# Attention with a long convolution in one kernel: score matmuls in tiles of four heads, a ring of three score bank pairs, and an instruction order planned at build time

## The chip, the cores and the metric

The kernel runs on one core of a Trainium2 chip. The metric is device time in microseconds (us). The engines are PE (TensorE, the matmuls), PEld (its weight loads), ACT (ScalarE), DVE (VectorE), POOL (GpSimd) and SP (SyncE, which issues most transfers). PSUM is the memory for the results of matmuls; both kernels use it as eight banks of 512 f32 columns. The "granted clock" is the share of full speed that TensorE was given in a stretch of time. In the traces of the kernels before and after, every record of it is 0.5 or 1.0; these are the low and the high clock below.

## The reference, cut to what matters

```python
# x: [2048, 640] bf16; 32 heads of 20; one key head and one value head for all
def A(q, k, v, shift_k, ssm_k, ssm_D):        # gated long convolution
    kv = shift_conv_4_taps(k, shift_k) * v
    y  = irfft(rfft(kv, 4096) * rfft(ssm_k, 4096))[:2048]   # causal convolution
    return q * (y + kv * ssm_D)
def B(x, wq, wk, wv, wo):                     # attention, 32 query heads
    p = softmax((x @ wq) (x @ wk)^T * 20 ** -0.5)           # 32 x 2048 x 2048
    return (p @ (x @ wv)) @ wo
g = sigmoid(sum(x * gate_w))
out = g * A(x, ...) + (1 - g) * B(x, ...)
```

The 32 x 2048 x 2048 exponentials are 1024 ScalarE instructions of 128 x 1024 elements, before and after. A head has 20 columns. A 21st carries a subtracted bound, so that no row maximum is needed, and the value matrix has a column of ones, so that the sum of the exponentials comes out of the output matmul. The trace lists a full matmul as `128*128` (rows and columns of the array), a score matmul as `21*128` and an output matmul as `128*32`. A score matmul therefore needs 21 of 128 rows. An output matmul needs 32 of 128 columns.

## The kernel before

Two heads form an item. There are two score slots (banks 0 to 3), two buffers ET for exponentials and two output banks (4 and 5). While the exponentials run, all other matmuls share banks 6 and 7.

```python
def QK(n):                                    # two heads: two row tiles
    ss = n % 2
    for hl in range(2):
        r = 2 * (hp % 2) + hl
        bankno = 2 * ss + hl
        op("pe", matmul(self.bank(bankno, 0, 512), A["kT4"][32*r:32*r+21, ...],
                        A[f"qT{g}"][32*r:32*r+21, ...], tile_position=(32 * r, 0)), ...)
# ... EXP(n): one activation over both banks of the slot into ET[n % 2]
# ... PV(n): two column-tiled matmuls, ET[n % 2] x vaug into bank 4 or 5
for n in range(N):                            # N = 1024
    EXP(n)
    if n + 2 < N:
        QK(n + 2)
    PV(n)
    # ... at the end of a head group: NORM, and OPROJ at the end of a query block
    self.step_credit += self.per_item         # convolution steps, evenly by weight
    self.step_credit = pull_steps(self.step_credit)
```

The convolution is done in blocks of 512 rows. Its steps take a spectrum of a block of kv again for each output block that needs it:

```python
for fc in range(4):
    for dl in range(b + 1):                   # output block b needs kv blocks b, b-1, ..., 0
        units.append((b, dri, d0, dn, fc, dl))
# ... each unit: X_unit(i = b - dl): 4 + 4 matmuls, two evacuations, then the products
```

All projections, the shifted product k * v and the gate came ahead of the first exponential. The spectra of ssm_k did too, in part.

## Time and profile before

| | before |
|---|---|
| time, median of 3 runs | 1838.95 us (1837.67 to 1840.55) |
| profiled span | 1834.4 us |
| first / last exponential starts | 247.1 / 1809.0 us |
| mean granted clock | 0.621 |

The main lines stand in the prediction below. Two more views help. The first is the chain of work that ended last, followed back from the end, as shares by engine:

```profile
PE 45%; ACT 17%; POOL 14%; DVE 13%; issue 9%; DMA 2%; SPq 0%; ACTq 0%; POOLq 0%; DVEq 0%
```

The second is a table by stretches: window, its length, then busy time (and number of instructions) of PE, PEld, DVE, ACT and POOL, the granted clock, the share of the DMA engines and GB/s.

```profile
0.00:247.00 247.00, 126.23 (x622) 48.87 (x622) 117.93 (x253) 56.15 (x81) 29.02 (x28) 0.70 0.13 39
247.00:647.00 400.00, 333.63 (x1455) 90.24 (x1455) 140.34 (x215) 246.67 (x246) 243.81 (x204) 0.67 0.10 29
647.00:1047.00 400.00, 355.71 (x1330) 79.90 (x1331) 99.76 (x143) 273.12 (x268) 82.57 (x105) 0.55 0.01 2
```

The chain is mostly PE. The stretches show how a kernel can be "bound by PE" and still lose time elsewhere. In the first 247 us no engine is much over half busy and no exponential runs. After that PE is 83 to 89% busy and ACT 62 to 68%.

### The profile page before, as it was taken

Reading aid. Unit: us, or ns where it says so; the run is one execution under the profiler, and the core shown is the slowest. Engines: PE = TensorE matmul, PEld = TensorE weight load, DVE = VectorE, ACT = ScalarE, POOL = GpSimd, SP = SyncE. Lnnn points to the kernel's source line nnn. Section 1 sums busy time; section 2 is a strip of 40 time slices with the busy share of each in tenths; the row PEclk is TensorE's granted clock in tenths of the full one; section 3 lists DMA queues with packets and bytes.
Section 4 is the critical chain, followed back from the end, with each engine's and each line's share of the span. In section 5 each row is a group of like instructions: output and inputs, shape, how many; then the busy total and the mean of one; then the engine's idle time right before and its main releaser. Section 6 shows DMA issues by size and latency. Waiting matters only on the chain.

```text
span 1834.4 us, 16661 instructions
## 1 busy us (share of the span) xinstructions
PE 1498.4 (82%) x6154; PEld 387.7 (21%) x6154; DVE 602.8 (33%) x1009; ACT 1091.1 (59%) x1105; POOL 599.2 (33%) x651
## 2 busy tenths in 40 slices
PE   3767258989968678999989888888989898898896
PEld 2212112212212122111111222221212211222221
DVE  6223842222355551212121233222315532323223
ACT  1213246756746437777767567666666466777674
POOL 1000199990056651102204044422234214524220
PEclk7787565655868676555555685655555756567556
DMA  3000222210000000000000000000000000000000
GB/s 109 1 0 1 79 72 72 72 45 10 4 1 1 0 8 8 0 1 0 1 0 1 8 8 1 1 0 0 1 1 1 15 1 0 1 1 1 1 1 15
DMA packets 22591, 24.70 MB, mean 13 GB/s; under 512 B 3316, under 2 KB 22382, under 8 KB 22510
## 3 DMA queue, kind: packets, MB, share of 16 engines
q1 hardware_dynamic: 22510, 23.64, 4.2%
q8 instruction: 48, 0.79, 0.2%
q14 instruction: 33, 0.27, 0.0%
HBM read 21.02 MB, written 2.62 MB: 13 GB/s over the span
## 4 chain that ended last, share of the span: by engine, by line
PE 45%; ACT 17%; POOL 14%; DVE 13%; issue 9%; DMA 2%; SPq 0%; ACTq 0%; POOLq 0%; DVEq 0%
ACT ET L1034 16%; PE ps L1024 13%; PE ps L1048 13%; PE ps L775 7%; POOL ksh_t L631 4%; POOL ksh_t L628 4%; PE ps L884 3%; PE ps L710 3%; POOL U L804 2%; DVE ps L1065 2%; POOL mtmp_pool L804 2%; POOL kv L635 1%; POOL ksh_t L624 1%; DVE accsb L1058 1%; PE ps L1075 1%
## 5 line engine op out<-in xcount | busy, mean ns | idle before, releaser
L1034 ACT ACTIVATE ET<-ps 128x1024 bf16<-128x1024 f32 x1024 | 1034.9, 1024 | 532.3 <-PE ps L1048 503.5
L1024 PE MATMUL ps<-qT,kT 21*128 21x512 bf16 x2048 | 562.0, 545 | 102.0 <-ACT ET L1034 71.9
L1048 PE MATMUL ps<-ET,vaug 128*32 128x512 bf16 x2048 | 569.0, 553 | 0.7 <-ACT ET L1034 0.7
L783 DVE CAST Xs<-ps 128x512 bf16<-128x512 f32 (+1 forms) x160 | 77.0, 489 | 500.5 <-PE ps L775 470.5
L804 POOL TENSOR_TENSOR mtmp_pool<-Xs,Kspec 128x128 f32<-128x128 bf16 (+3 forms) x189 | 146.7, 776 | 277.6 <-DVE U L804 265.9
L1024 PEld LDWEIGHTS ps<-qT,kT 21*128 21x128 bf16 x2048 | 102.8, 97 | 535.8 <-ACT ET L1034 433.3
L1048 PEld LDWEIGHTS ps<-ET,vaug 128*32 128x32 bf16 x2048 | 104.4, 99 | 390.5 <-issue 388.9
L897 POOL TENSOR_TENSOR yp<-yp,yp 128x512 bf16<-128x512 bf16 (+1 forms) x32 | 26.4, 825 | 458.3 <-DVE yp L888 457.6
L804 POOL TENSOR_TENSOR U<-U,mtmp_pool 128x128 f32<-128x128 f32 (+1 forms) x180 | 152.3, 846 | 14.1
L1065 DVE RECIPROCAL ps<-ps 128x512 f32<-128x512 f32 x32 | 107.7, 3367 | 21.6 <-PE ps L1062 21.6
L775 PE MATMUL ps<-kv,Tcos 128*128 128x512 bf16 (+1 forms) x320 | 88.0, 420 | 28.6 <-DVE Xs L783 22.6
L775 PE MATMUL ps<-kv,Tsin 128*128 128x512 bf16 (+1 forms) x320 | 89.3, 426 | 16.1 <-DVE oT L1067 14.6
L804 POOL TENSOR_TENSOR U<-Xs,Kspec 128x128 f32<-128x128 bf16 (+1 forms) x32 | 28.8, 901 | 205.5 <-DVE AB L846 204.2
L624 POOL TENSOR_TENSOR ksh_t<-kslab,w_all 128x640 bf16<-128x640 bf16 x16 | 22.8, 1423 | 212.1 <-DMA kslab<-in_A_k_dram 212.1
L246 DVE CAST Kspec<-ps 128x512 bf16<-128x512 f32 (+1 forms) x64 | 31.5, 491 | 173.6 <-PE ps L594 173.6
L248 ACT ACTIVATE qT<-ps 128x512 bf16<-128x512 f32 x32 | 18.6, 592 | 105.3 <-PE ps L710 89.3
L888 DVE CAST yp<-ps 128x512 bf16<-128x512 f32 (+1 forms) x32 | 15.7, 490 | 196.8 <-PE ps L884 196.8
L628 POOL TENSOR_TENSOR ksh_t<-kslab,w_all 128x640 bf16<-128x640 bf16 x48 | 68.7, 1431 | 2.5
L631 POOL TENSOR_TENSOR ksh_t<-ksh_t,ksh_t 128x640 bf16<-128x640 bf16 x48 | 67.6, 1409 | 3.8
L1058 DVE COPY accsb<-ps 128x512 f32<-128x512 f32 x32 | 22.1, 689 | 132.9 <-PE ps L1048 132.9
L1075 PE MATMUL ps<-wo,oT 128*128 128x512 bf16 (+1 forms) x256 | 49.7, 355 | 17.4 <-DVE outsb L1081 12.6
L884 PE MATMUL ps<-AB,Tcos 128*128 128x512 bf16 (+1 forms) x128 | 50.1, 429 | 15.1 <-DVE Xs L783 9.9
(142 smaller groups left out, 943.2 us busy)
## 6 DMA issues: line engine op xcount, KB each, us to landing
kslab<-in_A_k_dram SPq DMA_DIRECT2D x61, 160.0 KB
qx<-in_A_q_dram SPq DMA_DIRECT2D x2, 1280.0 KB
kstage<-in_A_ssm_k_dram SPq DMA_DIRECT2D x4, 640.0 KB
vslab<-in_A_v_dram SPq DMA_DIRECT2D x16, 160.0 KB
out_dram<-outsb SPq DMA_DIRECT2D x16, 160.0 KB
kstage<-in_B_wq_dram SPq DMA_DIRECT2D x2, 400.0 KB
wo<-in_B_wo_dram SPq DMA_DIRECT2D x32, 25.0 KB
w_all<-in_A_shift_k_dram SPq DMA_DIRECT2D x1, 640.0 KB
```

The lines of the kernel that those rows point to most:

```text
L628: op("pool", lambda e, s=slabs[j], j=j, tmpn=tmpn: e.tensor_tensor(A[tmpn][:, :], s[:, :], A["w_all"][:, j:4 * D:4], ALU.mult), reads=[ske ...
L631: op("pool", lambda e, accn=accn, tmpn=tmpn, dstn=dstn: e.tensor_tensor(A[dstn][:, :], A[accn][:, :], A[tmpn][:, :], ALU.add), reads=[accn ...
L710: op("pe", lambda e, g=g, sb=sb, dc=dc, bb=bb: e.matmul(self.bank(bb, 0, 512), A["wq_pad"][:, dc, g * 128:(g + 1) * 128], A["xT"][:, dc, s ...
L775: op("pe", lambda e, ncn=ncn: e.matmul(self.bank(bank, 0, dn), tab[:, ncn, fc * 128:(fc + 1) * 128], A["kv"][:, 4 * i + ncn, d0:d0 + dn], ...
L783: op("dve", lambda e: e.tensor_copy(A[f"Xs{slot}"][:, 0:dn], self.bank(bank, 0, dn)), reads=[("ps", bank)], writes=[("Xs", slot)], name="X ...
L804: op(eng, lambda e: e.tensor_tensor(out, a, b_, alu), reads=reads, writes=writes, name="mac")
L884: op("pe", lambda e, tab=tab, fc=fc, comp=comp, k=k: e.matmul(self.bank(bank, 0, dn), tab[:, fc, ci * 128:(ci + 1) * 128], srcbuf[:, comp, ...
L1024: op("pe", lambda e, r=r, g=g, I=I, j=j, bankno=bankno: e.matmul(self.bank(bankno, 0, 512), A["kT4"][32 * r:32 * r + 21, 128 * j:128 * j + ...
L1034: op("act", lambda e: e.activation(A[f"ET{slot}"][:, :], self.ps[:, 1024 * ss:1024 * ss + 1024], ACT.Exp, scale=scale), reads=[("ps", 2 * ...
L1048: op("pe", lambda e, slot=slot, hl=hl, j=j, rp=rp, first=first, last=last, pvb=pvb: e.matmul(self.bank(pvb, 0, 512)[32 * rp:32 * rp + 32, ...
L1065: op("dve", lambda e: e.reciprocal(self.bank(mb, 0, 512), self.bank(mb, 0, 512)), reads=[("ps", mb)], writes=[("ps", mb)], name="rinv")
L1075: op("pe", lambda e, g=g, ci=ci, bank=bank, n0=n0, nn=nn: e.matmul(self.bank(bank, 0, nn), A["oT4"][:, g, ci * 128:(ci + 1) * 128], A["wo4 ...
```

## The change

Its intent is to make ScalarE, which has work that cannot be removed, the only limit from beginning to end. It has these parts:

1. Scores and outputs are taken for four heads at a time, as four row tiles and four column tiles of the array.
2. The score banks form a ring of three pairs, with six ET buffers. One output bank (6) and one bank for all other matmuls (7) are left.
3. Each spectrum is taken once and kept. The width is 320 columns instead of 512 + 128.
4. The order of all other work is planned when the program is built. A list scheduler knows a cost for each instruction and places filler work where the attention leaves a gap.
5. Only two groups of query projections come before the first exponential. The k-shift, gate, convolution and later projections are fillers.
6. The reciprocal of the softmax sums goes over 128 x 16 elements after three small transfers, instead of 128 x 512.
7. The whole output projection comes after the scores.

The rewrite touches nearly every line, so the diff below is cut to its core.

```diff
-        def QK(n):
-            I, hp, j = items[n]
-            ss = n % 2
-            for hl in range(2):
-                r = 2 * (hp % 2) + hl
-                bankno = 2 * ss + hl
...
+        def pairs(u):
+            return (2 * u) % 3, (2 * u + 1) % 3
+        def QK(u):
+            Iu, g, j = u // 128, (u // 16) % 8, u % 16
+            pa, pb = pairs(u)
+            banks = (2 * pa, 2 * pa + 1, 2 * pb, 2 * pb + 1)
+            for r in range(4):
+                o = op("pe", lambda e, ...: e.matmul(self.bank(bk),
+                    T["kT4"][32 * r:32 * r + 21, 128 * j:128 * j + 128],
+                    T[f"qT{Iu % 2}"][32 * r:32 * r + 21, g, :], start=True, stop=True,
+                    tile_position=(32 * r, 0)), ..., 0.03 if r < 3 else 0.5, main=True, ...)
...
-        for n in range(N):
-            EXP(n)
-            if n + 2 < N:
-                QK(n + 2)
-            PV(n)
+        for u in range(lo, hi):                     # 512 units of four heads
+            EXP(u, 0)
+            if u + 1 < N:
+                QK(u + 1)
+            EXP(u, 1)
+            if u > 0:
+                PV(u - 1)
...
+    def pick_pe(self, t):                           # in the scheduler
+        ... # gap = time until the next attention group may start
+            if gr.ready <= t and gr.mms[0].cost <= gap + 0.25:
+                b = None
+                for x in gr.banks:
+                    if not self.bank_claimed[x] and not self.bank_busy[x] and self.bank_ready[x] <= t:
+                        b = x
+                        break
...
+    def oproj(self, I):
+                gr = self.group("op", pr + ci, banks=(7,) if I < 3 else (7, 6, 5, 4, 3, 2, 1, 0))
```

## The prediction

> **What bounds the kernel now.** I read the page first. Its part 1 gives the share of each engine and part 2 the same in 40 slices of 45.9 us.
>
> ```profile
> PE 1498.4 (82%) x6154; PEld 387.7 (21%) x6154; DVE 602.8 (33%) x1009; ACT 1091.1 (59%) x1105; POOL 599.2 (33%) x651
> ...
> PE   3767258989968678999989888888989898898896
> ...
> ACT  1213246756746437777767567666666466777674
> ...
> PEclk7787565655868676555555685655555756567556
> ```
>
> From slice 8 on PE is eight or nine tenths full and ACT six or seven, and the granted clock is mostly 0.5 to 0.6. So TensorE looks like the bound and ScalarE, which has the exponentials, has room. The groups say what that time is.
>
> ```profile
> L1034 ACT ACTIVATE ET<-ps 128x1024 bf16<-128x1024 f32 x1024 | 1034.9, 1024 | 532.3 <-PE ps L1048 503.5
> L1024 PE MATMUL ps<-qT,kT 21*128 21x512 bf16 x2048 | 562.0, 545 | 102.0 <-ACT ET L1034 71.9
> L1048 PE MATMUL ps<-ET,vaug 128*32 128x512 bf16 x2048 | 569.0, 553 | 0.7 <-ACT ET L1034 0.7
> ```
>
> The 1024 exponentials take 1035 us and ACT waits 503 us for PE between them. The 4096 attention matmuls cover 1131 us of PE: 2048 score matmuls of 545 ns cover 562 us only, so they run in pairs (1024 x 0.549 us). The source of one line tells that the first exponential starts at 247.1 us and the last at 1809.0 us. The span (1834) is thus a start of 247, a middle of 1563 and a tail of 25. The timeline shows the rhythm of the middle at the low clock (start, length, what):
>
> ```profile
> 1307.94 0.10 PEld L1024 LDWEIGHTS ps<-qT,kT 21*128 21x128 bf16 x2 [0.63 <-ACT ET L1034]
> 1307.95 0.61 PE L1024 MATMUL ps<-qT,kT 21*128 21x512 bf16 x2
> 1308.48 0.10 PEld L1048 LDWEIGHTS ps<-ET,vaug 128*32 128x32 bf16 x2 [0.44 <-issue]
> 1308.48 0.61 PE L1048 MATMUL ps<-ET,vaug 128*32 128x512 bf16 x2
> ...
> 1309.22 2.10 ACT L1034 ACTIVATE ET<-ps 128x1024 bf16<-128x1024 f32 x2 [0.25 <-PE ps L1048]
> ...
> 1310.11 1.89 PE L775 MATMUL ps<-kv,Tsin 128*128 128x512 bf16 x4
> ```
>
> A pair starts every 0.54 us, so an exponential of two heads costs PE 1.08 us: more than ACT's own pitch. Any convolution group (here 1.89 us for four matmuls) comes on top, and with two score slots and two ET slots ACT stops meanwhile. At the high clock (451 to 465 us, clock 1.00) a pair starts every 0.32 us and four 512-column matmuls of the Kspec group take 1.04 us.
>
> ACT's own pitch when nothing holds it is seen in its timeline:
>
> ```profile
> 466.23 11.58 ACT L1034 ACTIVATE ET<-ps 128x1024 bf16<-128x1024 f32 x12 [0.59 <-PE ps L1048]
> ```
>
> (11.58 - 1.02) / 11 = 0.96 us; a run of four in 3.86 us gives 0.945. The instructions overlap a little.
>
> [...] 820 to 828 us is 95% busy and still at 0.50, so busy time alone does not lift it here. [...]
>
> **The change part by part.**
>
> *Attention.* Same 4096 matmuls and 1024 exponentials, but in 512 units of four heads: four row-tiled score matmuls, two exponentials, four column-tiled output matmuls. I take a group of four as long as a pair, 0.54 us at the low clock. PE then spends 1.08 us per unit of 2 x 0.945 = 1.89 us of ACT, and 553 us in all instead of 1131. Three pairs of score banks and six ET buffers let the next unit's scores start when the first exponential of this one ends. From the trace: release ACT to PE 0.06 us, the matmuls 0.61, PE to ACT 0.13, and the exponential before it ends at 1.02, so the next may begin 1.82 us after its predecessor unit began, against 1.89 needed. It fits by 0.07 us when the clock is low and by 0.3 when high.
>
> *Other PE work in the middle*, by the instruction listing of the changed kernel: spectra 512 matmuls of 320 columns (before: 640 for X and 256 for Kspec, 205k + 82k columns, now 164k), inverse 256 x 320 (82k), query projection about 141 x 512 (72k; moved here from the start), norms 30 x 512 (15k), transposes 80 x 128 (10k). That is 343k columns, at 427 ns per 512 (four back to back start 0.42 apart in the trace) 286 us, or 0.56 us per unit, plus 0.11 us for each switch (a pair takes 0.54, not 0.427). Unit: 1.08 + 0.56 + 0.11 = **1.75 us of PE at the low clock against 1.89 of ACT**; at the high clock 0.64 + 0.28 + 0.11 = 1.03. The order listing agrees: 400 to 670 ns of fillers per unit in every stretch of 16 units, at most 854 in most single units. So ACT becomes the bound with a reserve of 7% at the low clock.
>
> *ACT* keeps only exponentials after the start. Middle without a stall: 1024 x 0.945 = 968 us.
>
> *DVE and POOL.* From rows of before (0.69 us for 512 f32, 0.43 for 512 bf16, 0.49 estimated for 320 from PSUM) my list for DVE sums to about 430 us: mac 144 ops 106, spectra evacuations 128 x 0.49 = 63, k-shift (moved from POOL) 53, norm 32 x 1.6 = 50, output and inverse 96 x 0.49 = 47, projections and squares 34, others 77. POOL: 152 x 1.55 + 24 x 0.8 + 32 x 0.75 = 280 us. Both are far below 968, so they cost only by coming late. The 3.37 us reciprocal (32 of them, 108 us) goes; a small one with three DMA hops takes its place, beside 16 units of attention.
>
> *Stalls* in the middle, my estimate: 32 changes of head group where the one output bank must be copied (0.69 us) before the next output matmul, some 0.3 us each, 10 us; units with three fillers at the low clock, about 130 x 0.1 = 13 us; fillers that wait for DVE to empty bank 7, and DVE waiting for a DMA in its fixed order, 17 us. Sum 40.
>
> *Start.* Exponentials began at 247 because all projections, k-shift and gate came first. Now only the first two query groups do. ACT does 12 sines (0.63), 13 + 6 evacuations (0.6), 4 small squares and two table loads (1.28) first, 23 us, after DMA issues and tables of some 6. The key maximum needs all of x (landed by 10.75 us before), then some ten short steps and a small DMA that sits in the queue behind about 7.3 MB of loads: at the 2.6 MB in 9 us seen for x, 25 us. First exponential at **36 us**, an estimate.
>
> *Tail.* The listing puts all 160 output-projection matmuls after the last score matmul, in 32 groups of 5, and 24 of them share bank 7. One such group is 5 x 0.14 + 0.3 until DVE starts + 0.49 + 0.06 = 1.5 us at the high clock (the tail of before ran at 0.85): 24 x 1.5 = 37. The last 8 use all banks, 6 us, and the last store lands 1.9 us after its issue (so waited DVE before). With the last output matmuls, **46 us** against 25 before. The last norm's DMA hops (some 13 us) hide behind the 24 groups.
>
> Sum: 36 + 968 + 40 + 46 = 1090, plus 4.5 by which the measured time exceeds the span before: **1095 us**.
>
> **The rivals.** *Four tiles do not run as one*: [...] Against it: pairs overlap fully here. *The fixed order loses to reality*: an engine that waits for a DMA or for DVE blocks everything behind it; at 0.3 us per unit this is 150 us, 1210 in all. For it speaks the single filler bank and the queue shared by all DMAs; against it that DVE is 45% busy and that DMA waits stand at few PE instructions. *The clock is high throughout*: denser groups may lift it, then stalls fall to 15 and the time to 1070. *The start is longer*, through the DMA queue: 60 instead of 36.
>
> **Range and chances.** The floor is 36 + 968 + 40 + 4.5, about 1050. Upwards, half of the second rival's stall or the first rival in part gives 1170. Range 1050 to 1170. Slower than before would need a failure of tiling and order together: faster 0.985, within 2% 0.01, slower 0.005.
>
> **What would show it.** Right: exponentials nearly without idle time before them, ACT above 88% busy, first one near 36 us, PE at 50 to 85%, four-tile groups of about 0.61 us (low) or 0.39 us (high) length, a tail of 46 us with PE waiting for DVE at the output projection. Wrong if ACT idles over 100 us before exponentials in the middle; the releaser then names the rival: score matmuls (tiles), DVE evacuations or DMA (order). A wrong start or tail shows in the first and last exponential.

## The result, and the profile after

The ratios here are, with their 95% intervals, taken over runs of the same rounds. They are therefore not quite the ratio of the quoted medians. The ratio in this table comes out as the mean of the ratios of all four rounds, the slow run included; the three fast runs alone give 1060.4 / 1837.5 = 0.577.

| | before | after |
|---|---|---|
| time, median of 4 runs | 1838.31 us (1833.95 to 1840.55) | 1064.2 us (1052.8 to 1068.87) |
| ratio | | 0.578 (0.574 to 0.583) |
| profiled span | 1834.4 us | 1058.3 us |
| first / last exponential starts | 247.1 / 1809.0 us | 34.0 / 991.4 us |
| mean granted clock | 0.621 | 0.605 |

The predicted time was 1095 us, in a range of 1050 to 1170, and faster by over 2%. The result lies in the range. One of the four runs, of 1068.87 us, was counted as slow; another of 1068.27 us was not.

The page of the kernel after, first the shares of the engines, then three rows of the 40 slices (now 26.5 us each), then the chain that ended last by engine:

```profile
PE 905.0 (86%) x5456; PEld 227.0 (21%) x5478; DVE 470.7 (44%) x804; ACT 976.2 (92%) x1062; POOL 293.3 (28%) x225
...
PE   6798998999899898898887789997998799977765
...
ACT  6899999999999999999999999999999999999500
...
PEclk9755555555655556656668775557555655588658
...
ACT 77%; PE 16%; DVE 4%; DMA 2%; issue 1%; ACTq 0%; SPq 0%
```

ACT stands at 9 from slice 3 to slice 37, and the chain is now ACT. PE is as busy as before in share, at the same half clock in most slices, but it no longer sets the pace. The groups of the same page say this in one line each (busy time, mean ns; idle time before and its cause):

```profile
L825 ACT ACTIVATE ET<-ps 128x1024 bf16<-128x1024 f32 x1024 | 954.5, 1059 | 4.7 <-PE ps L810 3.0
L810 PE MATMUL ps<-qT,kT 21*128 21x512 bf16 x2048 | 293.2, 563 | 114.1 <-ACT ET L825 109.3
L834 PE MATMUL ps<-ET,vaug 128*32 128x512 bf16 x2048 | 295.3, 566 | 0.2 <-ACT ET L825 0.2
```

The idle time of ACT before exponentials fell from 532 us to 4.7 us, and now the score matmuls wait for ACT. The 2048 score matmuls cover 293.2 us of PE, so a group of four covers 293.2 / 512 = 0.573 us where one matmul takes 0.563 us: the four tiles run as one. The timeline of ACT shows one run of 241 exponentials without a gap (start, length, what, number):

```profile
74.98 225.22 ACT L825 ACTIVATE ET<-ps 128x1024 bf16<-128x1024 f32 x241
```

No gap does not mean no wait. An exponential lasts at least 1.02 us, but when its input is ready it starts before the one ahead of it has ended. The starts of the single exponentials in the packed trace show this: 845 of the 1023 come 0.909 us after the start before on average (0.904 in the median). The other 178 come 0.95 us or more after it, 1.065 on average. Each of these 178 is the first of a unit of four heads, and nearly all start 0.06 us after the end of the unit's score matmuls, so they waited for the scores. Here is one of them (PE in the window 540 to 546 us, then ACT in the windows 543.0 to 543.05 and 544.3 to 544.35):

```profile
543.42 0.61 PE L810 MATMUL ps<-qT,kT 21*128 21x512 bf16 x4
...
543.01 1.10 ACT L825 ACTIVATE ET<-ps 128x1024 bf16<-128x1024 f32 x1
...
544.09 1.02 ACT L825 ACTIVATE ET<-ps 128x1024 bf16<-128x1024 f32 x1
```

The scores end at 544.03, and the exponential starts at 544.09, 1.08 us after the one before. The lost overlap of the 178 sums to 178 x (1.065 - 0.909) = 28 us. The page has only 4.7 us because it counts idle time, and a lost overlap leaves none. In these units the score matmuls started 0.23 us after the exponential that released them had ended (in the median), against 0.055 us in the others, because PE still worked on a matmul in front of them: a filler in 177 of the 178, and in 132 the third filler in a row. The scheduler's own rule, `cost <= gap + 0.25` in the cut above, lets a filler run 0.25 us into the time of the scores. That fits, but no run without this allowance was made.

A stretch of PE's timeline at the low clock shows one unit after another: four scores, four outputs, a filler from the convolution, then a short wait for ACT.

```profile
251.96 0.61 PE L810 MATMUL ps<-qT,kT 21*128 21x512 bf16 x4 [0.21 <-ACT ET L825]
252.50 0.62 PE L834 MATMUL ps<-ET,vaug 128*32 128x512 bf16 x4
253.05 0.45 PE L953 MATMUL ps<-kv,Tsin 128*128 128x320 bf16 x1
253.79 0.61 PE L810 MATMUL ps<-qT,kT 21*128 21x512 bf16 x4 [0.29 <-ACT ET L825]
```

The table by stretches (columns as before) separates the middle from the tail:

```profile
34.00:992.00 958.00, 840.61 (x5089) 196.41 (x5108) 420.10 (x676) 953.98 (x1025) 283.15 (x208) 0.59 0.11 33
992.00:1058.30 66.30, 41.96 (x164) 16.79 (x162) 20.00 (x37) 0.48 (x1) 0.00 (x0) 0.65 0.20 66
```

The tail of 66 us is the largest loss that is left. Its timeline shows a strict alternation between PE and DVE:

```profile
999.56 1.51 PE L1066 MATMUL ps<-wo,oTp 128*128 128x320 bf16 x5 [0.65 <-DVE outsb L1069]
1001.11 0.55 DVE L1069 SCALAR_TENSOR_TENSOR outsb<-ps,omgf,kv 128x320 bf16<-128x320 f32 x1 [1.61 <-PE ps L1066]
...
1001.72 1.51 PE L1066 MATMUL ps<-wo,oTp 128*128 128x320 bf16 x5 [0.65 <-DVE outsb L1069]
...
1040.29 0.85 PE L1066 MATMUL ps<-wo,oTp 128*128 128x320 bf16 x5 [0.65 <-DVE outsb L1069]
...
1041.79 0.85 PE L1066 MATMUL ps<-wo,oTp 128*128 128x320 bf16 x5 [0.65 <-DVE outsb L1069]
```

Every group of five output-projection matmuls waits until DVE has emptied the bank of the group before. A round trip is 2.16 us at the low clock and 1.50 us at the high clock. All 32 groups do this, although the list for the last block names eight banks. The reason is in the scheduler. It marks a bank as claimed when the attention first uses it, it never takes the mark back, and a filler group may only take an unclaimed bank.

### The profile page after: what moved, and what is told of

Its sections match the earlier page's. It is cut to its first block, busy times and chain, and to the rows that moved or that the text cites. A ratio compares the mean times of both kernels' runs of the same rounds, so it can differ in the third digit from the quotient of the medians.

```text
span 1058.3 us, 13504 instructions
## 1 busy us (share of the span) xinstructions
PE 905.0 (86%) x5456; PEld 227.0 (21%) x5478; DVE 470.7 (44%) x804; ACT 976.2 (92%) x1062; POOL 293.3 (28%) x225
## 4 chain that ended last, share of the span: by engine, by line
ACT 77%; PE 16%; DVE 4%; DMA 2%; issue 1%; ACTq 0%; SPq 0%
ACT ET L825 76%; PE ps L810 5%; PE ps L1066 3%; PE ps L751 3%; PE ps L834 3%; DVE outsb L1069 1%; DMA kslab<-in_A_k_dram 1%; PE ps L1040 1%; DMA rbc<-scr_d 0%; DVE gjunk L779 0%; DVE targ L643 0%; PE ps L682 0%; DVE kprod_dve L906 0%; DMA scr_d<-rcp 0%; DMA den<-acc 0%
## 5 line engine op out<-in xcount | busy, mean ns | idle before, releaser
L825 ACT ACTIVATE ET<-ps 128x1024 bf16<-128x1024 f32 x1024 | 954.5, 1059 | 4.7 <-PE ps L810 3.0
L810 PE MATMUL ps<-qT,kT 21*128 21x512 bf16 x2048 | 293.2, 563 | 114.1 <-ACT ET L825 109.3
L834 PE MATMUL ps<-ET,vaug 128*32 128x512 bf16 x2048 | 295.3, 566 | 0.2 <-ACT ET L825 0.2
L1002 POOL TENSOR_TENSOR Pp<-XK 128x640 f32<-128x640 bf16 x88 | 131.7, 1503 | 496.1 <-DVE XK L978 246.0
L1002 POOL TENSOR_TENSOR Pp<-Pp 128x640 f32<-128x640 f32 x64 | 102.0, 1595 | 5.0
L834 PEld LDWEIGHTS ps<-ET,vaug 128*32 128x32 bf16 x2048 | 56.2, 99 | 204.1 <-issue 195.2
L751 PE MATMUL ps<-xT,wq_pad 128*128 128x512 bf16 x139 | 67.2, 557 | 4.6 <-issue 2.3
L1002 DVE TENSOR_TENSOR Pd<-XK 128x640 f32<-128x640 bf16 x72 | 67.5, 944 | 1.2
L1040 PE MATMUL ps<-AB,Tcos 128*128 128x320 bf16 x128 | 49.1, 386 | 0.0
L1040 PE MATMUL ps<-AB,Tsinv 128*128 128x320 bf16 x128 | 49.0, 385 | 0.0
```

The costliest lines, as they stand in the source:

```text
L751: self.mm(gr, lambda e, bk, gi=gi, dc=dc: e.matmul(self.bank(bk), T["wq_pad"][:, dc, 128 * gi:128 * gi + 128], T["xT"][:, dc, 512 * I:512 ...
L810: o = op("pe", lambda e, r=r, Iu=Iu, g=g, j=j, bk=banks[r]: e.matmul(self.bank(bk), T["kT4"][32 * r:32 * r + 21, 128 * j:128 * j + 128], T ...
L825: op("act", lambda e, p=p, slot=slot: e.activation(T[f"ET{slot}"][:, :], self.ps[:, 1024 * p:1024 * p + 1024], ACT.Exp, scale=SCALE), [("p ...
L834: op("pe", lambda e, r=r, j=j, slot=slot: e.matmul(self.bank(6)[32 * r:32 * r + 32, :], T["vaug"][:, j, :], T[f"ET{slot}"][:, 512 * (r % 2 ...
L1002: self.op(eng, lambda e: e.tensor_tensor(out, a, c, alu), reads, writes, cst(n), prio=prio, port=True, name="mac")
L1040: self.mm(gr, lambda e, bk, tab=tab, fc=fc, comp=comp: e.matmul(self.bank(bk, HD), tab[:, fc, 128 * ci:128 * ci + 128], T["AB"][:, b, comp ...
```

## The experiments

All kernels gave correct results. The runs of one batch shared a chip and the runs of the kernel before. Batch 1 has the kernel after once more, the banks given back, the pairs and the plan for the high clock. Batch 2 has the shortened ring, the repeated spectra, the wrong DVE lengths and the plan between the two clocks. Batch 3 has the last two runs.

### The kernel after once more

No edit.

> The changed kernel unedited, as the measure for the other runs on the same chip. All theories: 1053 to 1069 us, as on record, ScalarE idle under 10 us between exponentials, tail (last exponential to end) 60 to 70 us.

Measured: 1060.38 us (1054.97 to 1067.61), ratio 0.577 (0.574 to 0.580). The profiled run had a span of 1065.8 us. Its first and last exponentials were at 33.6 and 991.2 us, almost exactly where they were in the first profile, so all of the 7.5 us between the two spans lies in the tail. Here the last group of the tail still runs at the low clock:

```profile
1060.61 1.51 PE L1066 MATMUL ps<-wo,oTp 128*128 128x320 bf16 x5 [0.65 <-DVE outsb L1069]
```

In the first profile the last 11 groups had the high clock, and 11 x (2.16 - 1.50) = 7.3 us. At least between these two runs, the spread of the kernel is the moment at which the clock rises in the tail.

### Banks given back in the tail

```diff
-                gr = self.group("op", pr + ci, banks=(7,) if I < 3 else (7, 6, 5, 4, 3, 2, 1, 0))
+                gr = self.group("op", pr + ci, banks=(7, 6, 5, 4, 3, 2, 1, 0))
...
+        for b, us in self.last_use.items():          # in place()
+            if self.bank_claimed[b] and all(x.placed for x in us):
+                self.bank_claimed[b] = False
+                self.bank_last[b] = list(us)
+                self.bank_ready[b] = max(x.end for x in us) + LAT
```

> One part changed: after the last score matmul the seven banks of scores and attention output are given to the output projection (before, a mark that is never taken back kept all 32 groups on bank 7). Theory (tail is 32 round trips matmuls, evacuation, matmuls on one bank): a group costs max(PE 1.33 us at the low clock or 0.70 at the high, DVE 0.55), so 22 to 43 us instead of 62, end to end 1024 to 1045 us. Rival (tail is held by the last norm's DMA hops and the stores, about 13 us + 2 per store on one queue): the tail stays above 58 us and the time within 8 us of the unedited kernel.

Measured: 1036.51 us (1035.71 to 1037.71), ratio 0.565 (0.563 to 0.567). The last exponential started at 992.1 us, so the middle is unchanged and the tail is about 41 us instead of 66. PE's timeline in the tail:

```profile
993.83 8.20 PE L1072 MATMUL ps<-wo,oTp 128*128 128x320 bf16 x45
1006.23 6.74 PE L1072 MATMUL ps<-wo,oTp 128*128 128x320 bf16 x35 [4.20 <-DVE outsb L1075]
1015.85 6.03 PE L1072 MATMUL ps<-wo,oTp 128*128 128x320 bf16 x40 [2.87 <-DMA oTp<-scr_o]
1023.78 6.03 PE L1072 MATMUL ps<-wo,oTp 128*128 128x320 bf16 x40 [1.90 <-DMA oTp<-scr_o]
```

Nine groups now run back to back, where each had waited for DVE. The bank round trips were the cause of most of the long tail. The clock in this tail is 0.92, against 0.65 before, and the time spreads over 2 us instead of 13. Part of the gain is this clock: the 21 round trips at the low clock would have been 21 x 0.66 = 14 us shorter at the high one. The run does not separate it from the round trips themselves. What remains are three waits: for DVE, which itself stands behind a broadcast of the last reciprocals, and twice for loads of oTp.

### Pairs of heads, with ring and planned order kept

```diff
...
-            if u + 1 < N:
-                QK(u + 1)
+            if u + 1 < N:
+                QK(u + 1, (0, 1))
+            if u > 0:
+                PV(u - 1, (0, 1))
+            if u + 1 < N:
+                QK(u + 1, (2, 3))
             EXP(u, 1)
...
-                PV(u - 1)
+                PV(u - 1, (2, 3))
```

> The four-head groups alone undone: scores and outputs go in pairs again (2 score matmuls, 2 output matmuls, 2, 2), with the ring of three bank pairs, the list scheduler and the single spectra kept. Theory A (the four tiles in one go are what takes PE off the path): four pairs of 0.54 us, 2.16 us of PE per unit at the low clock, 1106 us, plus 286 us of other matmuls and 56 of switches: the middle becomes 1400 to 1500 us, the whole 1500 to 1650, and ScalarE waits for PE over 400 us. Theory B (ring and order do it): under 1200 us.

Measured: 1677.19 us (one run, so its state is unknown), slightly above the range of the theory. The groups and a stretch of the table by windows:

```profile
L817 ACT ACTIVATE ET<-ps 128x1024 bf16<-128x1024 f32 x1024 | 1047.1, 1023 | 477.5 <-PE ps L808 421.7
```

```profile
540.00:640.00 100.00, 100.00 (x370) 19.09 (x368) 9.34 (x17) 92.87 (x92) 0.00 (x0) 0.50 0.04 13
```

ACT is idle 478 us again, and PE is busy 1456 us instead of 905. Between 540 and 640 us PE has no idle time at all and ACT still advances only 92 exponentials in 100 us. In most units an exponential starts 1.08 us after the one before, which is the 2.16 us per unit of the theory. The four-head groups are thus what takes PE off the critical path, and they are worth 1677 - 1060 = 617 us in this design. Not all of that is the pace: 400 of the 478 us lie in eight waits of 8 to 146 us, in which the fillers that found no gap are worked off. PE is busy for only 154 of 270 us in the two longest (661 to 787 and 1091 to 1235 us), because its groups stand behind DVE, which has to empty bank 7. The ring, the planned order and the other parts together, without them, gain 1838 - 1677 = 161 us. The early start accounts for more than that: the first exponential moves from 247 to 34 us, while the tail of this kernel (from its last exponential at 1557 us) is 118 us instead of 25.

### The score ring shortened from three bank pairs to two

```diff
-            return (2 * u) % 3, (2 * u + 1) % 3
+            return 0, 1
```

> The ring of three score bank pairs alone undone: every unit of four heads uses the same two pairs, so its score matmuls wait for both exponentials of the unit before. Theory A (the ring hides the score matmuls behind an exponential): a unit needs 1.02 + 0.94 us of exponentials + 0.06 + 0.61 + 0.13 for the score matmuls at the low clock, 2.76 us, middle 1413 us, whole 1450 to 1500; at the high clock 2.5 us, 1320 to 1370. ScalarE idles 0.5 to 0.9 us in every unit before an exponential, for PE scores. Theory B (the order and the tiles alone suffice): under 1120 us.

Measured: 1460.72 us (one run, state unknown). The first theory held. All waits of ACT are for the scores:

```profile
ACT ET L825 <- PE ps L810: 399.6, 512, 2.4
```

These are 512 waits, one per unit, and 399.6 / 512 = 0.78 us each: the time of a score group and its two signals, which can't start before the second exponential of the unit before has ended. The ring hides this. It is worth 400 us, even though PE is only 61% busy here.

### The planner told that matmuls take the time of the high clock

```diff
-    return 0.02 + 0.8e-3 * n
+    return 0.02 + 0.42e-3 * n
...
-    ... 0.03 if r < 3 else 0.5, ...
+    ... 0.03 if r < 3 else 0.24, ...                 # scores and outputs
```

> Only the scheduler's idea of a matmul's length is changed (0.42 ns a column as at the high clock instead of 0.8): the order gets about twice the filler matmuls between two score groups, all of them done by unit 360 of 512, and three of four output projections move ahead of the last exponential. Theory (PE at the low clock has only some 12% to spare, the order is right because it was planned with the low clock): in the first 360 units PE needs 2.05 to 2.2 us against 1.87 of ScalarE, ScalarE idles 60 to 120 us there, the tail shrinks by about 40: 1080 to 1140 us. Rival (denser PE work lifts the clock, reserve is larger than it looks): no idle ScalarE, 1015 to 1035 us.

Measured: 1053.48 us (1053.04 and 1053.92), ratio 0.574 (0.571 to 0.577). Neither expectation held. The table by stretches shows what happened:

```profile
334.00:434.00 100.00, 80.01 (x608) 27.75 (x608) 69.13 (x105) 96.47 (x105) 42.02 (x31) 0.85 0.08 23
...
834.00:934.00 100.00, 63.39 (x440) 12.09 (x440) 5.86 (x11) 100.00 (x111) 0.00 (x0) 0.50 0.05 16
```

The planner packed the fillers early and densely, and there the clock rose to 0.85. PE's real speed came close to the wrong plan, so ACT was idle only 25.9 us in all. When the fillers were used up, attention alone ran at 0.50, with ACT 100% busy. The last exponential came at 1008.1 us instead of 991.2, but the tail shrank to 43 us. This order went with another clock (0.714 in the mean, against 0.605 in the kernel after), so the cost that a planner should assume depends on the plan that it makes.

### Each spectrum taken as often as before

```diff
-                            for nc_ in range(4):
+                            for nc_ in list(range(4)) * (NB - i if kind == "X" else 1):
...
+                                for _ in range(NB - i - 1):
+                                    self.evac(gr, "dve", ... T["junk"] ...)
```

The added work is 384 matmuls of 320 columns and 96 evacuations, placed by the same scheduler. The copied `junk` isn't used. The edit is shown without the start and stop flags that it does not touch.

> The part 'no repeated spectra' alone undone in cost: the spectra of the kv blocks are computed 4, 3, 2, 1 times as before (384 matmuls of 320 columns and 96 evacuations of 0.49 us more, the repeats thrown away; the result stays right). Theory A (PE has little to spare in the middle, so the extra 102 us at the low clock displace other filler work into the tail): 83 inverse matmuls stand after the last score matmul, in the tail 10 groups of some 2.8 us, and ScalarE idles in a burst of 280 spectra matmuls: 1090 to 1140 us. Theory B (PE's waiting absorbs it, and denser work lifts the clock): within 12 us of the unedited kernel.

Measured: 1194.7 us (1187.03 to 1195.65), ratio 0.649 (0.645 to 0.652). This is 134 us more than the kernel after, and more than expected. ACT's waits show that it is not an even shortage of PE:

```profile
ACT ET L826 <- PE ps L811: 128.7, 6, 111.9
```

One wait of 111.9 us, from 761 to 873 us, makes nearly all of it. In this stretch PE is busy for only 72 of 112 us. It works through inverse transforms, spectra and the next block's query projection, and nearly every group waits 0.6 us or more for DVE to empty bank 7. Nine waits of 1.1 to 2.9 us follow the thrown-away evacuations, which the edit puts in a row behind one group; they make 17 of the 40 us in which PE is idle there. When the filler load exceeds what the gaps hold, the rest piles up at the next query block, and there the single filler bank makes it slow. Dropping the repeats is worth some 134 us in this design, less what the row of evacuations adds. The run does not say what a planner with other priorities, or a second filler bank, would make of the larger load.

### The planner told that DVE is faster than it is

```diff
-    return 0.16 + 1.04e-3 * n
+    return 0.6 * (0.16 + 1.04e-3 * n)
-    return 0.16 + 0.52e-3 * n
+    return 0.6 * (0.16 + 0.52e-3 * n)
```

> Only the scheduler's idea of VectorE's lengths is changed, to 0.6 of the true ones; the work is the same. The order then counts on evacuations of bank 7 that come 0.2 to 0.4 us too early. Theory A (the fixed order costs nothing because its lengths are the true ones): PE waits for VectorE in front of some 250 groups, the scores behind it come late, ScalarE idles 20 to 80 us, 1080 to 1140 us. Theory B (the slack of PE per unit, some 0.2 us, and six ET buffers forgive it): ScalarE idle under 10 us and within 10 us of the unedited kernel.

Measured: 1072.99 us (1068.93 to 1074.26), ratio 0.583 (0.580 to 0.586). Neither theory held in full. ACT was idle 22.6 us before exponentials, against 4.7, and the last one started at 1013.5 us, 22 us later than with the true lengths. The tail was 58 us instead of the 67 and 75 of the two profiles; 28 of the 160 output-projection matmuls had moved ahead of the last exponential. So the order does matter: knowing the lengths of DVE's work is worth some 20 us in the middle, of which 12.6 us (1073.0 against 1060.4) show in the time. A 40% error in these lengths costs no more than that.

### Banks given back, and a plan between the two clocks

```diff
-    return 0.02 + 0.8e-3 * n
+    return 0.02 + 0.7e-3 * n
-    ... 0.03 if r < 3 else 0.5, ...
+    ... 0.03 if r < 3 else 0.44, ...
```

> Both repairs: the banks are given back after the last score matmul, and the planned matmul length is 0.7 ns a column and 0.53 us a group of four instead of 0.8 and 0.59, so that the fillers spread evenly (530 to 770 ns of low-clock work per unit) and three of four output projections run before the last exponential. Theory (what is left is start 34, 1024 exponentials at 0.936 us, and a tail of one norm with its DMA hops, 8 groups and a store): tail 26 to 34 us, ScalarE idle under 15 us, 1018 to 1032 us. Rival (the fuller units stall ScalarE as under the high-clock order): ScalarE idle 25 us or more and over 1036 us.

Measured: 1049.37 us (1047.27 to 1050.2), ratio 0.571 (0.568 to 0.573). The banks given back alone had 0.565. The rival held. ACT was idle 25.0 us before exponentials, 21.7 of them in 76 waits for the scores, and the last exponential started at 1011.2 us instead of 992.1. The fuller units went with a mean clock of 0.676 (0.599 with the banks given back alone) and the scores were late all the same. The pessimistic plan of the kernel after is the better one.

### Banks given back, and a key for each quarter of oTp

In the tail above, the four quarter loads of oTp ran one after another, because the scheduler's dependences know oTp by a single key. A load waited for the landing of the one before.

```diff
-                     writes=[("oTp", I % 2)], nbytes=163840, prio=-800, name="ld_oT")
+                     writes=[("oTp", I % 2, dd)], nbytes=163840, prio=-800, name="ld_oT")
...
-                        start=(kc == 0), stop=(kc == NDC - 1)), [("oTp", I % 2), "wo"], c_mm(HD))
+                        start=(kc == 0), stop=(kc == NDC - 1)), [("oTp", I % 2, d) for d in range(4)] + ["wo"], c_mm(HD))
```

> As e1_tail_banks, and the four quarter loads of oTp have a key each, so that the plan no longer makes one wait for the landing of the one before. Theory: in the tail of e1 PE waited 2.9 us and 1.9 us for oTp (and 4.2 us for DVE, which stood behind the broadcast rbc); with overlapping loads the first two waits go, the tail falls from 40 to about 35 us, and the time from 1036.5 to 1028 to 1033 us. Rival: the last head group's own hops (den, rcp, rbc, oTn, scr_o, then oTp) set the end, the loads were hidden behind it or share the same DMA time, and the time stays within 1034 to 1038 us. The middle should not change: last exponential near 991 us.

The kernel with only the banks given back ran beside it on the same chip:

> e1_tail_banks unedited, on the same chip as e9_split_keys, as its measure: 1034 to 1039 us.

Measured: 1031.75 us (1031.22 to 1033.03) against 1036.65 us (1034.87 to 1039.12). The ranges of the five runs do not overlap. The ratios to the kernel before are 0.563 and 0.566. The last exponential started at 992.3 us. PE's tail in the timeline now has no wait for oTp:

```profile
993.99 8.28 PE L1072 MATMUL ps<-wo,oTp 128*128 128x320 bf16 x45
...
1006.39 0.69 DVE L882 TENSOR_TENSOR oTn<-acc,rbc 128x512 bf16<-128x512 f32 x1 [5.04 <-DMA rbc<-scr_d]
...
1007.60 12.79 PE L1072 MATMUL ps<-wo,oTp 128*128 128x320 bf16 x75 [5.34 <-DVE outsb L1075]
...
1020.60 6.03 PE L1072 MATMUL ps<-wo,oTp 128*128 128x320 bf16 x40 [0.21 <-DVE outsb L1075]
```

The gain is 5 us. The wait for DVE is still there: in its fixed order DVE waits 5.0 us for the broadcast of the reciprocals, while results that it could empty stand in the banks. This is the fastest version, and it beats both kernels.

## Why the prediction was right, and where its terms were off

The mechanism held. The sum of 1095 us was too high by 39 us for ACT's pitch and by 12 for the stalls, and too low by 21 for the tail. That the time lies in the range is in part luck: with the banks given back, which the prediction counted on for its last 8 groups, the kernel takes 1036.5 us, below the floor of 1050 us. The spans below are the profiled run's; its time was 1060.1 us.

| step of the prediction | predicted | measured |
|---|---|---|
| first exponential | 36 us | 34.0 us |
| middle without a stall | 968 us | 929 us |
| stalls in the middle | 40 us | 28 us (4.7 us of them idle time) |
| tail | 46 us | 67 us |
| time above the span | 4.5 us | 1.8 us |

The middle runs from the first exponential's start to the last one's, 957.4 us. The 929 us are 1023 x 0.9085, the mean distance of the starts that did not wait for scores; the rest are the 28 us worked out above.

- **Four tiles take as long as a pair.** Right: 0.573 us per group of four, against 0.549 us per pair before. The trace before shows pairs alone, so the step to four was the author's estimate. The rival, that they do not run as one, fell; no run measured such a group. The kernel of pairs (1677 us) shows that the whole result hangs on this step.
- **PE has a reserve of 7% at the low clock.** Right on average: PE was busy 840.6 us of 958 in the middle, 88%, at a mean clock of 0.59, and 93 us of 100 between 134 and 234 us, where the clock was 0.52. In single units there was none: in 178 of 511 PE was late with the scores. The rival of a clock that is high throughout fell. The repeated spectra, 384 matmuls more, no longer fitted. Of the signs that the prediction named, one missed narrowly: PE's share of the whole span is 86%, not 50 to 85%.
- **The ring lets the next scores hide, with 0.07 us to spare.** Right: in the units whose scores were not late, the exponential started 0.134 us after they ended (in the median), where the late ones needed 0.06, so some 0.07 us were to spare. With two pairs of banks each unit waits 0.78 us. With so little to spare, a filler that ran over by more than that reached ACT.
- **ACT's pitch.** This is a mis-sized term, by 39 us. The distance of two starts was predicted as 0.945 us, "when nothing holds it", from short runs of four and twelve in the profile before. Without late scores it is 0.909 us in the mean. The runs in the profile before were held: the 93 starts there that come 0.93 to 1.01 us after the one before stand nearly all 0.13 us behind the end of the output matmuls that give back their ET buffer. Why the second exponential of a unit comes after 0.904 us in 284 units and after 0.920 in 227 stays open.
- **Stalls.** The estimate was 40 us: changes of head group (10), units with three fillers (13) and waits for bank 7 or a transfer (17). Measured are 28 us, nearly all of the second kind: fillers that made the scores late in 178 units, by about 0.16 us each, and in 177 of these the score group ran at the low clock. Of the 178 units 132 had three fillers, where the prediction had put 130 such units at 0.1 us. The changes of head group do not stand out, since the late units lie evenly over the 16 units of a group. The sum is nearly of the right size, but its parts are not. With wrong DVE lengths the same count gives 48 us, so a good order is what keeps the stalls small; the rival that had the fixed order lose 150 us was far off.
- **Tail.** This is the term that was too small, by 21 us, with two wrong inputs: "The last 8 use all banks, 6 us" and a high clock for all groups. All 32 groups went through bank 7, because the claim on the other banks was never given back, and in the profiled run 21 of them ran at the low clock with a round trip of 2.16 us. Giving the banks back took 24 us off the time (1060.4 to 1036.5). The list of eight banks in the source had been read as what happens; the listing of instructions by engine does not show banks. Counting the round trips on bank 7 again for all 32 groups gives 21 x 2.16 + 11 x 1.50 = 62 us, nearly the whole tail.
- **Start.** Right within 2 us; its parts were not checked one by one.

What stays open: the runs do not separate what makes the clock rise. Dense fillers went with 0.85, attention alone with 0.50, but no run changes only the kind of matmul at a fixed busy time. The gain that is left in the order of DVE in the tail (some 5 us) was not tried, and neither was a plan without the allowance of 0.25 us for fillers.

## What to carry to other kernels

When two engines alternate on one resource, look for the engine whose work cannot shrink, make every other engine cheaper than its pitch, and give it a buffer more, so that its next input is made while it works; here four heads per group and the third pair of banks were each worth several hundred us. A planned order holds well if its lengths come from a trace at the slow clock. Little idle time does not show that an engine never waits: compare the distance of its starts with the shortest that occur. After the bound has moved, look at the ends: a forgotten claim on a bank and one key for four loads cost 24 and 5 us, and the source did not look slow in either place.

## What the traces show of the clock, the tiles and the engines

- In the kernel of pairs PE was 100% busy from 540 to 640 us at a granted clock of 0.50; with the fillers packed it was 80% busy at 0.85 (334 to 434 us). In the kernel before it was 95% busy from 820 to 828 us at 0.50. Busy time alone does not decide the clock here.
- A group of four score matmuls covered 0.573 us and one matmul 0.563 us, which by these lengths is an estimate of 4 x 0.563 / 0.573 = 3.9 times as fast as four in a row. But full matmuls of 512 columns start 0.42 us apart at the low clock, and groups of four 0.54 us apart, which is 4 x 0.42 / 0.54 = 3.1. No run here makes the same four score matmuls one after the other.
- Groups of row tiles and of column tiles that alternate at the low clock start 0.54 us apart, while full matmuls of 512 columns start 0.42 us apart. That is about 0.12 us per group; no run shows its cause.
- In the kernel after, the 72 two-input products of 640 columns on DVE took 0.76 to 0.83 us alone (51) or when they began before a product on POOL (8). The 13 that took longer, 0.98 to 2.15 us, all began while a product on POOL was running, and ended 0.68 to 0.69 us after it. No run changes this alone.
